# A Fourier-mixing layer with a gated feed-forward: first loads on GpSimd's queue, exponent clamps on GpSimd, 20 products of ones, and a planner with new costs and keys

## The chip, the cores and the metric

One core of one Trainium2 chip runs the kernel. The metric is the device time in microseconds. Three runs of the kernel before took 1538.30, 1540.07 and 1543.28 us, a median of 1540.07.

## What is computed

x is 8 images of 3136 rows by 256 channels. Each image is transformed along its rows, mixed across channels by a complex matrix, soft-thresholded and transformed back. The 25088 rows then go through a feed-forward of width 1024.

```python
def _attn_ref(x, w_r, w_i, b_r, b_i):
    X = np.fft.rfft(x, axis=1)
    Yr = Xr @ w_r - Xi @ w_i + b_r
    Yi = Xr @ w_i + Xi @ w_r + b_i
    Yr = np.sign(Yr) * np.maximum(np.abs(Yr) - lam, 0.0)      # Yi alike, lam = 0.01
    y = np.fft.irfft(Yr + 1j * Yi, n=x.shape[1], axis=1)

def _moe_ref(x, w_in, w_out, g_ln):
    h = x @ w_in
    solu = h * softmax(h)
    ln = (solu - mu) / np.sqrt(var + 1e-06) * g_ln
    return ln @ w_out
```

## The kernel before, in words

The transform of length 3136 = 98 x 32 is done in two stages with a twiddle between them. For image 0, `fwd1_plain` (L778) takes x in eight chunks of 98 x 1024, multiplies each by the 98 x 98 matrix `fa_s` (fp32, two products of 512 columns a chunk, two instructions a product), copies the results out of PSUM on ScalarE and stores them to DRAM (`s1f`). The four even chunks are loaded on SyncE's queue (tiles `u`), the four odd ones on ScalarE's (tiles `xw`). VectorE takes each chunk's largest magnitude (`peaks`). `x_scale` (L664) turns the eight peaks into one scale: a reduce (`top`), a transpose by TensorE, a reduce (`v`), and in `spread` (L683) a product with a row of ones that puts the value on all partitions, and small VectorE operations that end in the scale `sc[:, 4:]`.

`load_bin` (L818) reads the stored result back in another layout (for image 0 into the `xw` tiles), ScalarE casts it to fp16 and VectorE makes the low half (tile `bin`); `fwd2` (L923) is the second stage with filters `fb`; `mix_first` (L974) multiplies by the mixing matrix (`w_hi`, `w_lo`, 12 products of 512 columns for each of 12 units); `threshold` (L1014) and two GpSimd subtractions (`y<-yt,yc` and `yl<-y,yh`) follow; `inv1` (L1038) is the first inverse stage with filters `gb`, stored to DRAM; `inv2` (L1097) reads it back and makes the rows of the feed-forward (`ring_hi`, `ring_lo`). Of each 128 rows, a head (`ph`, softmax), a turn (cast, transposes by DMA) and a tail (`po`, output) make the result. Image 1's first stage is plain as well; images 2 to 7 use a folded one (`fwd1_fold`).

The feed-forward's weights arrive as 64-bit words, since the host hands them over as doubles. `load_wide` (L619) loads 512 of them per partition and rebuilds fp32: mask the exponent (tile `lh`), two clamps of it (`lh<-lh`, written as `ex`), merge it with the sign (`ll<-u,lh`), build the mantissa (`junk`), and one GpSimd product of the two. There are eight such loads: four for `w_in` (`moe_w_in`, L1315) and four for `w_out` (`moe_w_out`, L1345). `power_of_two` (L1330) makes a scale from their peaks.

The mixing weights w_r and w_i are four loads of 128 x 256 fp32 (tile `zt`), held after an earlier copy in the plan. The constants `gs_s`, `fs_s`, `iaf_s`, `fq_s`, `ia_s` and the filters are loaded by `load_after` (L649) on SyncE's queue. `load` (L594) loads `fa_s`; two more loads on SyncE bring the bias rows. Twelve products of ones run at the start while nothing else is there.

No instruction is issued at once. `Plan` records every operation, weighs it (`weigh`, L408: a length, and for a transfer the bytes on a shared bus), and `order` (L459) simulates the five engines: whenever one is free it takes, among the operations that could start within 50 ns of the earliest, the one with the lowest key. The program is then issued in the order of the simulated starts; on each engine it runs in that order. A key is that of the stage and image (`KEYS`, with a step per unit), plus an offset for stage and image (`SHIFT`) and one for the tile written (`ROLE`). `hold` delays an operation in the plan alone; on the chip only real data and buffers are waited for. `x_scale` of image 1 is the ninth step (n = 8) of stage `a1`: its key before is -75.67 + 8 x 10.825.

Of the kernel before, what the change touches and what calls it, by code (L numbers as in the profile page):

```python
# [18 lines left out]
ALU = mybir.AluOpType  # L19
# [225 lines left out]
class Banks:  # L245
# [49 lines left out]
    "b4": -0.33, "b6": 1.62, "a5": 2.05, "b5": -2.17, "b2": 2.33, "a4": 2.62, "b3": -3.91, "a6": -6.82,  # L295
    "a7": -10.33, "a2": -10.77, "a3": 12.99, "b1": 20.66, "b0": -70.35,
# [3 lines left out]
    "head/ph": -0.29, "w_in1/u": 0.37, "b/bin": 0.51, "a/both": 0.58, "head/u": -0.59, "b/Xl": 0.68,  # L300
    "a/av": 0.68, "a/peaks": 1.29, "b/yl": 1.86, "b/Dgb2": 1.92, "w_in0/u": 2.5, "inv2/last_hi": -3.37,
    "a/hsb": 3.92, "weights/u": 3.99, "a/v": 4.16, "a/un": 4.33, "a/pf": -5.05, "head/m": 5.41,
    "w_out0/lh": 5.94, "b/pf": -6.04, "b/Xh16": -6.25, "w_in0/Du": -6.43, "b/yt": 6.86, "a/xw1": -7.25,
    "turn/junk": 7.47, "b/Xs": -7.58, "inv2/last_lo": -8.25, "b/Dgb3": 8.73, "b/y": -10.12, "b/zs": 10.35,
    "w_in1/ll": 10.7, "w_out/o": 12.33, "b/bin_s16": -13.08, "w_out/wout": 17.67, "turn/ll": 24.16,
    "head/a": 36.36, "a/sc": -39.48, "b/zout": -44.76,
# [19 lines left out]
class Op:  # L326
    def __init__(self, engine, stage, role, seq):
        self.engine, self.stage, self.seq = engine, stage, seq
        self.key = key_of(*stage) + SHIFT.get("".join(map(str, stage[:2])), 0) + ROLE.get(f"{stage[0]}/{role}", 0)
        self.calls, self.length, self.moved, self.tiles = [], 0.0, 0.0, []  # L330
        self.needs, self.next, self.start, self.end, self.half, self.port = set(), [], None, None, False, False
# [7 lines left out]
class Plan:  # L339
# [7 lines left out]
    PACE = 1.006  # L347
# [60 lines left out]
    def weigh(self, op, name, args, kw, ins, outs):  # L408
        if name == "dma_start":
# [3 lines left out]
            op.length += 1600.0 if cross else 430.0  # L413
            op.moved += 1500.0 if cross else size / 270.0
# [8 lines left out]
        else:  # L423
# [11 lines left out]
            if op.engine == "gpsimd" and name == "tensor_scalar":  # L435
                each = 1.15
# [6 lines left out]
            op.length += self.CALL[op.engine] + big * each + max(scalars, 0) * self.SCALAR[op.engine]  # L443
# [15 lines left out]
    def order(self):  # L459
        ready = {e: [] for e in self.ENGINES}  # L460
        free = dict.fromkeys(self.ENGINES, 0.0)
        waits, bus, half, port = {}, 0.0, False, 0.0
# [16 lines left out]
        def may_start(op):  # L479
            at = max(free[op.engine], op.at, port if op.port else 0.0, bus - self.BACKLOG if op.moved else 0.0)  # L480
            taken = {}
            for t in op.tiles:
                if t.owner is None:
                    k = t.kind
                    n = len(k.placed) + taken.get(k, 0)
                    taken[k] = taken.get(k, 0) + 1
                    if turn.get(t, n) != n:
                        return np.inf
                    n -= k.bufs
                    if n >= 0:  # L490
# [76 lines left out]
def fft_mix_solu_kernel(ctx: ExitStack, tc, x, w_r, w_i, b_r, b_i, w_in, w_out, g_ln, fa, fq, none, iaf, fb, fs, gb, gs, ia, out):  # L567
# [35 lines left out]
    for r, v in enumerate((b_r, b_i)):  # L603
        nc.sync.dma_start(bias_row[:, r], v.unsqueeze(0))
# [14 lines left out]
    def load_wide(dst, src, before=None):  # L619
# [17 lines left out]
        nc.vector.tensor_scalar(ex, ex, least, -least, ALU.max, ALU.add)  # L637
        nc.vector.tensor_scalar(ex, ex, float(255 << 20), 8.0, ALU.min, ALU.mult)
# [10 lines left out]
    def load_after(t, src, before):  # L649

        nc.hold(before)
        nc.sync.dma_start(t, src)
# [11 lines left out]
    def x_scale(b):  # L664
# [16 lines left out]
        nc.vector.tensor_scalar(sc[:, 4:], sc[:, :1], S_SCALE, None, ALU.mult)  # L681
# [136 lines left out]
    def load_bin(b, g):  # L818
# [11 lines left out]
        if b == 0 and g == 0:  # L830
            for to, src in ((gs_s, gs), (fs_s, fs), (iaf_s, iaf), (fq_s, fq), (ia_s, ia)):
                load_after(to, src, raw[0, 0])
        if b == 0:
            load_after(fb_s[g], fb[:, g * QG : (g + 1) * QG], raw[0, g - 1] if g else done[0, NCH - 1])
# [642 lines left out]
```

## Time and profile before

| | us |
|---|---|
| median of three runs | 1540.07 |
| the profiled execution's own time | 1535.88 |
| its span, first to last instruction | 1533.9 |
| TensorE busy | 1489.9 |
| VectorE busy | 1226.8 |
| ScalarE busy | 1166.3 |
| GpSimd busy | 1084.9 |

PE is TensorE's products and PEld its weight loads, DVE is VectorE, ACT ScalarE, POOL GpSimd, SPq the queue on SyncE that issues transfers. Nearly every instruction carries the line of one recording helper (L457), so instructions are told apart by their tiles, written out<-in. All PSUM tiles are parts of one tensor, `store`. PEclk is TensorE's granted clock as a share of 2.4 GHz. A product's start is when it began; because products overlap, their steps are better read from the starts than from the durations.

### The profile page before, as it was taken

How to read it: one execution, taken by the hardware profiler on the slowest of the kernel's cores; microseconds unless marked ns; L12 is line 12 of the kernel's file. 1: busy time of each engine (PE TensorE's matmuls, PEld its weight loads, DVE VectorE, ACT ScalarE, POOL GpSimd, SP SyncE). 2: the span in 40 equal slices, each digit the busy share in tenths (PEclk: the TensorE clock that was granted, in tenths of full speed). 3: DMA queues.
4: the chain of work that ended last, by engine and by line, in shares of the span. 5: the costliest groups of instructions: out<-in, count | busy, mean ns of one | idle time of the engine just before them, and what ended most of it. 6: DMA issues, size and time to landing. Idle time of an engine off the chain costs nothing.

```text
span 1533.9 us, 40789 instructions
## 1 busy us (share of the span) xinstructions
PE 1489.9 (97%) x15471; PEld 1036.4 (68%) x15471; DVE 1226.8 (80%) x2571; ACT 1166.3 (76%) x2134; POOL 1084.9 (71%) x1351
## 2 busy tenths in 40 slices
PE   6979999999999999999999999999999999999998
PEld 3436677676666777766677677667777777776666
DVE  4888989888888898888889898777886877776664
ACT  5767877778778877778677787777887877677775
POOL 0555787778767778677876887758887788765665
PEclk8989999999999999999999999999999999999999
DMA  8779868987899889998799998897865955687766
GB/s 242 214 231 227 172 153 178 201 174 176 161 233 197 194 191 207 182 190 183 151 218 200 218 194 194 193 203 153 163 137 125 190 116 132 129 172 147 142 120 120
DMA packets 527312, 273.14 MB, mean 178 GB/s; under 512 B 426752, under 2 KB 505068, under 8 KB 527056
## 3 DMA queue, kind: packets, MB, share of 16 engines
q1 hardware_dynamic: 526668, 268.94, 81.8%
q8 instruction: 121, 1.98, 0.6%
q10 hardware_dynamic: 448, 1.61, 0.4%
q14 instruction: 75, 0.61, 0.1%
HBM read 84.71 MB, written 82.97 MB: 109 GB/s over the span
## 4 chain that ended last, share of the span: by engine, by line
PE 51%; DVE 3%; ACT 1%; issue 1%; POOL 1%; DMA 1%; SPq 0%; DVEq 0%; ACTq 0%; POOLq 0%
PE store L457 51%; DMA xw<-in_x_dram 1%; POOL ll L457 1%; DVE m L457 1%; DVE u L457 0%; ACT u L457 0%; ACT lh L457 0%; DVE bin L457 0%; DVE peaks L457 0%; DMA th<-lh 0%; SPq L457 0%; DVE yt L457 0%; DVE xw L457 0%; POOL r L457 0%; ACT junk L457 0%
## 5 line engine op out<-in xcount | busy, mean ns | idle before, releaser
L457 POOL TENSOR_TENSOR ll<-u,lh 128x1024 f16<-128x1024 f32 x196 | 422.6, 2157 | 162.8 <-ACT lh L457 147.6
L457 PE MATMUL store<-wout,th 128*128 128x256 f16 x3136 | 374.8, 273 | 5.0 <-DVE Xl L457 1.5
L457 PEld LDWEIGHTS <-th 128*128 128x128 f16 x3136 | 303.0, 98 | 65.1 <-issue 10.6
L457 DVE TENSOR_REDUCE m<-store 128x1 f32<-128x1024 f32 x196 | 239.1, 1220 | 94.1 <-PE store L457 93.2
L457 DVE SCALAR_TENSOR_TENSOR u<-store,ch,u 128x1024 f32<-128x1024 f32 x196 | 250.9, 1280 | 74.0 <-ACT u L457 71.8
L457 ACT CAST lh<-u 128x1024 f16<-128x1024 f32 x196 | 205.8, 1051 | 121.3 <-DVE u L457 66.4
L457 PE MATMUL store<-win_hi,ring_hi 128*128 128x512 f16 x768 | 291.3, 379 | 3.5 <-DVE u L457 2.9
L457 PE MATMUL store<-win_low,ring_lo 128*128 128x512 f16 x768 | 291.0, 379 | 0.0
L457 PE MATMUL store<-win_lo,ring_hi 128*128 128x512 f16 x768 | 291.0, 379 | 0.0
L457 ACT ACTIVATE u<-store,m,hsb 128x1024 f32<-128x1024 f32 x192 | 231.6, 1206 | 76.8 <-DVE m L457 73.5
L457 PEld LDWEIGHTS <-ring_hi 128*128 128x128 f16 x1536 | 148.2, 98 | 148.3 <-issue 11.5
L457 ACT ACTIVATE junk<-u,su 128x1024 bf16<-128x1024 f32 x196 | 226.6, 1156 | 3.4 <-DVE u L457 3.3
L457 PE MATMUL store<-wout,tl 128*128 128x256 f16 x1568 | 203.4, 273 | 1.7 <-DMA tl<-ll 1.7
L457 PEld LDWEIGHTS <-tl 128*128 128x128 f16 x1568 | 151.6, 98 | 27.7 <-issue 3.4
L457 PE MATMUL store<-w_hi,Xh 128*128 128x256 f16 (+1 forms) x584 | 165.4, 283 | 3.5 <-ACT Xh L457 1.3
L457 PE MATMUL store<-w_hi,Xl 128*128 128x256 f16 (+1 forms) x584 | 165.3, 283 | 0.6 <-DVE Xl L457 0.3
L457 PE MATMUL store<-w_lo,Xh 128*128 128x256 f16 (+1 forms) x584 | 165.2, 283 | 0.0
L457 POOL TENSOR_TENSOR y<-yt,yc 128x512 f32<-128x512 f32 (+1 forms) x104 | 128.9, 1241 | 29.3 <-ACT yt L457 26.3
L457 PEld LDWEIGHTS <-Xh 128*128 128x128 f16 x1168 | 112.7, 98 | 37.1 <-issue 11.0
L457 PEld LDWEIGHTS <-ring_lo 128*128 128x128 f16 x768 | 75.1, 98 | 90.7
L457 POOL TENSOR_TENSOR yl<-y,yh 128x512 f16<-128x512 f32 x96 | 112.8, 1179 | 18.5 <-ACT yh L457 18.1
L457 ACT ACTIVATE o<-store,r 128x256 f32<-128x256 f32 x196 | 93.3, 477 | 40.3 <-PE store L457 36.9
(178 smaller groups left out, 2468.8 us busy)
## 6 DMA issues: line engine op xcount, KB each, us to landing
s<-av SPq DMA_DIRECT2D x48, 512.0 KB
zt<-s SPq DMA_DIRECT2D x56, 392.0 KB
s<-zout SPq DMA_DIRECT2D x42, 512.0 KB
xw<-in_x_dram SPq DMA_DIRECT2D x48, 384.0 KB
bin<-s SPq DMA_DIRECT2D x72, 256.0 KB
out_dram<-o SPq DMA_DIRECT2D x128, 96.0 KB
out_dram<-o SPq DMA_DIRECT2D x136, 64.0 KB
out_dram<-o SPq DMA_DIRECT2D x128, 32.0 KB
```

The costliest lines, as they stand in the source:

```text
L457: getattr(engine, name)(*args, **kw)
```

## The change

The matrix `fa_s`, the two bias rows, the mixing weights, the five constants and the first filter block are issued on GpSimd's queue. Two of the four exponent operations of each wide load run on GpSimd. Twenty more products of ones are put on TensorE once image 0's scale is there. The planner counts at most eight transfers in flight on the hardware queues, has other lengths for transfers and for GpSimd's operations, and all keys differ.

```diff
-    "fa": -300, "bias": -243.29, "start": 0, "warm": -200, "plain": -200, "weights": -203.16, "consts": -100,
-    "groups": 0, "x0": -175.82, "y0": -51.96, "b0": -115.32, "b0s": 4.277, "w_in0": -161.15, "w_in1": -112.71,
-    "w_in": -109.53, "w_out0": -71.07, "w_out": -17.01, "mix": 116.28, "pads": -69.29, "a1": -75.67,
-    "a1s": 10.825, "a2": 18.06, "a2s": 1.034, "a": 0.49, "b1": -21.98, "b1s": 1.959, "b": 2.06, "bs": 1.538,
-    "inv2": -85.41, "turn": 153.65, "tail": 3.96, "as": 1.842,
+    "fa": -300, "bias": -279.1, "start": 0, "warm": -200, "plain": -200, "weights": -170.64, "consts": -100,
+    "groups": 0, "x0": -159.35, "y0": -57.88, "b0": -127.06, "b0s": 2.121, "w_in0": -171.39, "w_in1": -140.45,
+    "w_in": -126.15, "w_out0": -114.06, "w_out": -71.7, "mix": 30.93, "pads": -77.8, "a1": -130.39,
+    "a1s": 16.887, "a2": -19.92, "a2s": 1.248, "a": -1.85, "b1": -27.4, "b1s": 1.388, "b": -1.43, "bs": 1.393,
+    "inv2": -132.6, "turn": 153.08, "tail": 3.75, "as": 1.384, "again": -154.07,
 SHIFT
-    ... "a3": 12.99, "b1": 20.66, "b0": -70.35,
+    ... "a3": 11.28, "b1": 30.66, "a1": -37.21, "b0": -65.91,
 ROLE (37 offsets in place of 37 others)
 Plan
+    LANES = 8
+    LAND = 2300.0
-    PACE = 1.006
+    PACE = 1.003
 weigh, a transfer
-            op.length += 1600.0 if cross else 430.0
-            op.moved += 1500.0 if cross else size / 270.0
+            soft = op.engine == "gpsimd"
+            op.length += 1400.0 if cross else 1000.0 if soft else 530.0
+            op.moved += 700.0 if cross else size / 270.0
+            op.lane = not soft
 weigh, a GpSimd operation
+            if op.engine == "gpsimd" and name == "tensor_scalar":
+                each = 345.0 if big == 1 else 140.0 + big * 1.15
 may_start
+            if op.lane and len(lands) >= self.LANES:
+                at = max(at, lands[-self.LANES])
 order
-                op.end = bus + 2000.0
+                op.end = bus + self.LAND
+                if op.lane:
+                    lands.append(op.end)
 load; the bias rows
-        nc.sync.dma_start(t, src)
+        nc.gpsimd.dma_start(t, src)
-        nc.sync.dma_start(bias_row[:, r], v.unsqueeze(0))
+        nc.gpsimd.dma_start(bias_row[:, r], v.unsqueeze(0))
 load_wide
-        nc.vector.tensor_scalar(ex, ex, least, -least, ALU.max, ALU.add)
-        nc.vector.tensor_scalar(ex, ex, float(255 << 20), 8.0, ALU.min, ALU.mult)
+        nc.gpsimd.tensor_scalar(ex, ex, least, -least, ALU.max, ALU.add)
+        nc.gpsimd.tensor_scalar(ex, ex, float(255 << 20), 8.0, ALU.min, ALU.mult)
 load_after
-        nc.sync.dma_start(t, src)
+        (queue or nc.sync).dma_start(t, src)
 x_scale, image 0
-        nc.vector.tensor_scalar(sc[:, 4:], sc[:, :1], S_SCALE, None, ALU.mult)
+        nc.hold(nc.vector.tensor_scalar(sc[:, 4:], sc[:, :1], S_SCALE, None, ALU.mult))
+        nc.at("again")
+        pw = banks.tile("po")
+        with nc.together():
+            for k in range(20):
+                nc.tensor.matmul(pw[:, :P], ones, ones, start=k == 0, stop=k == 19)
 load_bin: gs, fs, iaf, fq, ia, and fb of block 0
-                load_after(to, src, raw[0, 0])
+                load_after(to, src, raw[0, 0], nc.gpsimd)
 the mixing weights
-            load_after(w3[h][:, j], w[h * P : (h + 1) * P], done[0, 3])
+            load_after(w3[h][:, j], w[h * P : (h + 1) * P], done[0, 3], nc.gpsimd)
```

## Rows read from the trace of the kernel before

**Rows 1.** The page: TensorE's busy time, share of the span, instructions.

```profile
PE 1489.9 (97%) x15471; PEld 1036.4 (68%) x15471; DVE 1226.8 (80%) x2571; ACT 1166.3 (76%) x2134; POOL 1084.9 (71%) x1351
```

**Rows 2.** Stretches of the run: busy time by engine, granted clock, DMA.

```profile
core 0: us, PE busy (x) PEld busy (x) DVE busy (x) ACT busy (x) POOL busy (x), PEclk, DMA share, GB/s
6.47:26.87 20.40, 19.42 (x45) 7.92 (x46) 10.11 (x10) 11.33 (x22) 2.79 (x4) 0.92 0.87 264
26.87:45.00 18.13, 8.25 (x79) 3.70 (x79) 12.89 (x37) 11.33 (x21) 0.00 (x0) 0.63 0.77 228
45.00:96.00 51.00, 48.10 (x689) 24.00 (x686) 43.81 (x72) 40.20 (x79) 35.67 (x29) 1.00 0.77 231
96.00:108.00 12.00, 3.02 (x26) 0.73 (x9) 11.58 (x26) 8.19 (x15) 3.92 (x4) 0.66 0.77 251
130.00:900.00 770.00, 755.53 (x8200) 532.06 (x8206) 664.23 (x1374) 602.11 (x1108) 577.96 (x712) 1.00 0.90 189
900.00:1520.00 620.00, 620.00 (x6278) 443.31 (x6261) 465.29 (x999) 476.09 (x858) 456.10 (x590) 1.00 0.76 156
```

**Rows 3.** TensorE's timeline, first 41 us: start, duration, instruction, [idle before <-releaser].

```profile
1.34 4.36 PE L457 MATMUL store<-ones 128*128 128x128 f32 x24 [1.34 <-DVE mhalf L457]
6.47 1.96 PE L457 MATMUL store<-xw,fa_s 98*98 98x512 f32 x4 [0.77 <-DMA xw<-in_x_dram]
...
11.06 3.65 PE L457 MATMUL store<-u,fa_s 98*98 98x512 f32 x4 [0.72 <-DMA u<-in_x_dram]
14.98 1.96 PE L457 MATMUL store<-u,fa_s 98*98 98x512 f32 x4 [0.26 <-DMA u<-in_x_dram]
...
28.46 0.62 PE L457 MATMUL store<-v,ones 1*128 1x1 f32 x4 [1.12 <-DVE v L457]
35.62 0.29 PE L457 MATMUL store<-fb,bin 64*128 64x64 f16 x4 [6.54 <-ACT bin L457]
36.94 1.35 PE L457 MATMUL store<-fb,bin 64*128 64x64 f16 x44 [1.03 <-DVE bin L457]
...
39.87 0.63 PE L457 MATMUL store<-w_lo,Xh 128*128 128x512 f16 x1
40.30 0.62 PE L457 MATMUL store<-w_hi,Xl 128*128 128x512 f16 x1
```

**Rows 4.** SyncE's queue, timeline of issues: start, time to issue, transfer.

```profile
0.72 0.44 SPq L457 DMA_DIRECT2D fa_s<-in_fa_dram  x1
...
1.80 6.76 SPq L457 DMA_DIRECT2D u<-in_x_dram  x4
...
26.91 0.34 SPq L457 DMA_DIRECT2D s1f<-tl  x1
...
30.46 2.04 SPq L457 DMA_DIRECT2D xw<-s1f  x4
```

**Rows 5.** Stretches of 2 us around the first hole, columns as in rows 2.

```profile
30.00:32.00 2.00, 0.00 (x0) 0.00 (x0) 2.00 (x7) 2.00 (x7) 0.00 (x0) 0.91 0.16 48
32.00:34.00 2.00, 0.00 (x0) 0.00 (x0) 1.43 (x4) 1.85 (x7) 0.00 (x0) 0.50 0.91 314
...
44.00:46.00 2.00, 2.00 (x52) 1.13 (x51) 0.75 (x1) 0.14 (x1) 0.00 (x0) 0.68 0.86 233
```

**Rows 6.** TensorE's timeline from 94 to 118 us.

```profile
108.01 0.32 PE L457 MATMUL store<-ident,top 98*1 98x98 f32 x1 [6.58 <-DVE top L457]
108.12 6.30 PE L457 MATMUL store<-xw,fa_s 98*98 98x512 f32 x8
```

**Rows 7.** VectorE's timeline: image 0's last scale; the clamp nearest to `top`.

```profile
29.32 0.15 DVE L457 TENSOR_SCALAR sc<-sc 128x1 f32<-128x1 f32 x1
...
105.34 0.41 DVE L457 TENSOR_SCALAR lh<-lh 128x512 uint32<-128x512 uint32 x1
```

**Rows 8.** Tile `lh` from 40 to 131 us: ns min/median/max, first and last start.

```profile
L457 DVE TENSOR_SCALAR lh<-lh x16: 410/414/834, 49.2 to 110.6; 128x512 uint32<-128x512 uint32 x16
```

**Rows 9.** GpSimd's groups over the run: busy us, mean ns, idle before.

```profile
L457 POOL TENSOR_TENSOR y<-yt,yc 128x512 f32<-128x512 f32 x96 | 122.5, 1277 | 29.2 <-ACT yt L457 26.3
...
L457 POOL TENSOR_SCALAR yc<-yt,sc 128x512 f32<-128x512 f32 x84 | 68.1, 812 | 24.2 <-DVE yt L457 19.3 <-DVE ch L457 3.5 <-DVE un L457 0.8
```

More of the change, by code (lines that the diff above doesn't have):

```diff
@@ L292 @@
+    "groups": 0, "x0": -159.35, "y0": -57.88, "b0": -127.06, "b0s": 2.121, "w_in0": -171.39, "w_in1": -140.45,
+    "w_in": -126.15, "w_out0": -114.06, "w_out": -71.7, "mix": 30.93, "pads": -77.8, "a1": -130.39,
+    "a1s": 16.887, "a2": -19.92, "a2s": 1.248, "a": -1.85, "b1": -27.4, "b1s": 1.388, "b": -1.43, "bs": 1.393,
+    "inv2": -132.6, "turn": 153.08, "tail": 3.75, "as": 1.384, "again": -154.07,
 }
 SHIFT = {
-    "b4": -0.33, "b6": 1.62, "a5": 2.05, "b5": -2.17, "b2": 2.33, "a4": 2.62, "b3": -3.91, "a6": -6.82,
@@ L296 @@
-    "a7": -10.33, "a2": -10.77, "a3": 12.99, "b1": 20.66, "b0": -70.35,
+    "b5": -0.34, "a6": 2.88, "a7": 6.98, "b2": 7.05, "b4": 7.45, "a5": 7.96, "a4": 9.2, "a3": 11.28, "b1": 30.66,
+    "a1": -37.21, "b0": -65.91,
 }
 ROLE = {
-    "head/ph": -0.29, "w_in1/u": 0.37, "b/bin": 0.51, "a/both": 0.58, "head/u": -0.59, "b/Xl": 0.68,
-    "a/av": 0.68, "a/peaks": 1.29, "b/yl": 1.86, "b/Dgb2": 1.92, "w_in0/u": 2.5, "inv2/last_hi": -3.37,
-    "a/hsb": 3.92, "weights/u": 3.99, "a/v": 4.16, "a/un": 4.33, "a/pf": -5.05, "head/m": 5.41,
@@ L303 @@
[L303 to L306, printed above, removed]
+    "tail/po": 0.15, "head/ph": -0.17, "w_in0/u": 0.4, "b/Dxw0": 0.46, "b/bin": 0.6, "a/sc": 0.72,
+    "turn/r": -0.79, "head/u": -1.18, "a/v": -1.49, "head/m": 1.55, "w_in1/lh": 1.69, "head/ch": -1.89,
@@ L307 @@
+    "a/bias_y": 1.98, "a/both": 2.12, "b/Xl": -2.31, "a/top": 3.09, "a/xw0": 3.16, "weights/u": -4.1,
[3 rows of a table added]
+    "w_in1/ll": 20.29, "a/peaks": 25.23, "head/a": 36.79, "b/zout": -55.1,
 }
@@ L330, in __init__ @@
         self.calls, self.length, self.moved, self.tiles = [], 0.0, 0.0, []
-        self.needs, self.next, self.start, self.end, self.half, self.port = set(), [], None, None, False, False
+        self.needs, self.next, self.start, self.end, self.half, self.port, self.lane = set(), [], None, None, False, False, False
     def touch(self, tile):
@@ L434, in weigh @@
                 each = 2.12
-            if op.engine == "gpsimd" and name == "tensor_scalar":
-                each = 1.15
             if op.engine == "vector" and sbuf and name in ("tensor_scalar", "tensor_copy") and big > 1:
@@ L442, in weigh @@
                 op.port = True
-            op.length += self.CALL[op.engine] + big * each + max(scalars, 0) * self.SCALAR[op.engine]
+            each = self.CALL[op.engine] + big * each + max(scalars, 0) * self.SCALAR[op.engine]
+            if op.engine == "gpsimd" and name == "tensor_scalar":
+                each = 345.0 if big == 1 else 140.0 + big * 1.15
+            op.length += each
             if "accum_out" in kw and op.engine == "scalar":
@@ L461, in order @@
         free = dict.fromkeys(self.ENGINES, 0.0)
-        waits, bus, half, port = {}, 0.0, False, 0.0
+        waits, bus, half, port, lands = {}, 0.0, False, 0.0, []
         for op in self.ops:
@@ L647, in fft_mix_solu_kernel, with load_after @@
     s1 = {}
-    def load_after(t, src, before):
+    def load_after(t, src, before, queue=None):
         nc.hold(before)
-        nc.sync.dma_start(t, src)
+        (queue or nc.sync).dma_start(t, src)
     xw = [const.tile([P, 2 * C1], F32, name=f"xw{i}") for i in range(2)]
@@ L831, in load_bin @@
             for to, src in ((gs_s, gs), (fs_s, fs), (iaf_s, iaf), (fq_s, fq), (ia_s, ia)):
-                load_after(to, src, raw[0, 0])
+                load_after(to, src, raw[0, 0], nc.gpsimd)
         if b == 0:
-            load_after(fb_s[g], fb[:, g * QG : (g + 1) * QG], raw[0, g - 1] if g else done[0, NCH - 1])
+            load_after(fb_s[g], fb[:, g * QG : (g + 1) * QG], raw[0, g - 1] if g else done[0, NCH - 1], None if g else nc.gpsimd)
             load_after(gb_s[g].rearrange("p u r t m -> p u (r t) m"), gb[:, g * QG // 2 : (g + 1) * QG // 2].rearrange("p u r t m -> p u (r t) m"), raw[b, g])
```

3 rows, old and new, of the table ROLE are left out of this document.

## The prediction

> **What bounds the kernel now.** I read the page first, then stretches of the run, then TensorE's own rows where it stands still, then the queue or engine that it waits for. On the page TensorE is busy for 1489.9 of 1533.9 us [rows 1]. So about 44 us are all that any reordering can win from waiting, plus what TensorE loses while its granted clock is at half. The stretches show where those are [rows 2]. From 900 to 1520 us TensorE never waits. From 130 to 900 it waits 14.5 us. The rest lies in the first 108 us, in two holes. In the first (26.87 to 45.00) it is busy 8.25 of 18.13 us at a mean clock of 0.63; in the second (96 to 108) 3.02 of 12 us at 0.66. After each hole the time lost is not made up, because TensorE has work queued behind it without a break; what is saved there comes off the end nearly one for one.
>
> The first hole is a round trip. TensorE's last product before it is the spread of image 0's scale at 28.46; the next starts at 35.62, when ScalarE has cast the first block read back from DRAM [rows 3]. That block's load is issued at 30.46, after the last store at 26.91 has landed [rows 4]. The granted clock falls in the middle of the hole: 0.91 from 30 to 32 us, 0.50 from 32 to 34, and 0.68 only from 44 to 46 [rows 5], that is from 2.4 to 1.2 GHz until some 9 us after work resumed.
>
> The second hole is TensorE's queue held up by one instruction. The transpose of image 1's peak (`top`) waits 6.58 us for VectorE and starts at 108.01; eight first-stage products stand behind it and run at half clock [rows 6].
>
> **The change, part by part.** The sum is made against the profiled execution, 1535.88 us (span 1533.9 and 2.0 outside it); the median of the three runs shown, 1540.07, lies 4.2 above it. I put the differences on the median.
>
> *Loads on GpSimd's queue.* The DFT matrix and two bias rows leave SyncE's queue, so its first load of x is issued at 0.72 in place of 1.80 [rows 4]: 1.08 us sooner. TensorE waits for that load at 11.06 and for the next at 14.98, and runs without a break from there to the end of the stage [rows 3]. At 11.06 the four products also take 3.65 us, against 1.96 for the same four at 14.98. At best the stage gains 1.08 + 1.69 = 2.8 us. Against it: the mixing weights (4 loads of 128 KB) move to GpSimd's queue too. Their hold on an earlier copy orders the plan only and is no wait on the chip; nothing stands before them in GpSimd's queue but the matrix and the biases, so they go out while x is still coming. 524 KB at the stage's 264 GB/s [rows 2] are 2.0 us. I take the middle of -2.8 and +2.0: **-0.4**. The matrix itself: GpSimd's queue shows no load in this trace. On SyncE it is issued at 0.72 and first needed at 6.47 [rows 4, 3]. The move costs between 0 (it still lands in time) and 5.7 us (it takes that long once more); as the product of 6.47 waits for x, I take 0. The five later constants, the first filter block and the weights are 10 issues fewer on SyncE; I take 0, since SyncE waits from the issue at 26.91 to 30.46 for the store to land, whatever stood before. Were that cover gone, they would be worth an issue of some 0.4 us each.
>
> *Ones products.* 20 fp32 products of 128x128 are 40 instructions; 24 such take 4.36 us at the start [rows 3], so these take 7.27. They are held by the last scale of image 0, which the trace shows at 29.32 to 29.47 [rows 7]. They end near 36.74. TensorE's queue is in order, so the four products of 35.62 wait behind them, and all of image 0's chain behind those; but the next 44 wait for VectorE until 36.94 anyway [rows 3]. I price the delay at +0.1 (bounds 0 and +1.1, the whole 36.74 - 35.62). In return the clock should still be full when the mix starts: its products follow each other at 0.43 us now (39.87, 40.30 [rows 3]), at half clock; twelve of them at full clock save 12 x 0.215 = 2.6. Bounds: 0 if the chain behind is bound elsewhere, 4.1 if all of the 8.25 us that TensorE is busy in that hole [rows 2] were halved. Sum of this part **-2.5**.
>
> *Clamps on GpSimd.* Eight wide loads each give up two VectorE clamps; the sixteen have a median of 0.414 us [rows 8]: 6.6 us off VectorE. The last of four such clamps ahead of `top` starts at 105.34 [rows 7], and VectorE is busy 11.58 of the 12 us of that hole [rows 2], so `top` comes 4 x 0.41 = 1.6 us sooner. On GpSimd I take 0.81 us each, from its threshold operation of the same shape; its two-input subtract of 1.28 is the upper bound [rows 9]. That is 13 us (at most 20) in stretches where GpSimd is idle 15.3 us before 96 us and 8.1 us in the hole [rows 2]. The price is a new wait: VectorE's sign merge now waits for two GpSimd operations, and behind it stand the low halves and peaks for which TensorE waits; on GpSimd, the subtractions of image 0's mix stand behind the clamps, and the inverse stage waits for these. I cost those at 0, since GpSimd's idle time covers them.
>
> *Plan and keys.* The new costs and keys reorder all five queues. What that gives cannot be read from rows; only its bounds can. In the second hole the whole loss is 9.0 us of idle and 2.9 us of half clock (the eight products of 108.12 take 6.30, at full clock about 8 x 0.43 [rows 6, 3]), 11.9 together. The last step of image 1's front, which makes `top`, moves from key +10.9 (-75.67 + 8 x 10.825) to -32.5, ahead of the first heads, which suggests a smaller hole. The weights of the output layer move ahead as well (-71 to -114), which keeps VectorE full. Bounds for this hole: -11.9 and +1.6 (below, the port). I take the clamps' 1.6 and half of the 4.94 us that remain of the wait: **-4.1**. In the long stretch after 130 us I take 0, with bounds of -14.5 (all waiting there gone) and +13.2 (two waits like the 6.58).
>
> Sum: -0.4 - 2.5 - 4.1 + 0 = **-7.0**, so 1533.1 us for the median (1528.9 against the profiled execution). A difference of 0.3%, 4.6 us, is about what a measurement of this kernel tells from no change.
>
> **The rivals.** (1) *The second hole closes.* The keys put enough work before `top`, and its wait and half clock go altogether: -6.6 - 2.9 in place of -4.1; with the full lead of the first load this is -2.8 - 2.5 - 9.5 = -14.8, **1525.3**. For it: VectorE alone holds that wait. Against: work that could fill it also waits for VectorE or for image 0's own round trip.
>
> (2) *GpSimd's clamps block VectorE.* The clamp on VectorE varies from 0.410 to 0.834 us [rows 8]: something doubles it at times. If each of the four clamps before `top` holds VectorE for its 0.81 us, VectorE loses 3.2 us and gains 1.6: +1.6 in place of -4.1, sum -1.3, **1538.8**. The Trainium skill states such a rule (SBUF — State Buffer, section Who interferes with whom): VectorE's two-port and two-input SBUF instructions and GpSimd share a port pair as an exclusive lock, and the second to issue blocks. The spread of 0.410 to 0.834 agrees with it, but the median of 0.414 says that it is rare so far.
>
> (3) *Slower: the new order opens holes in the long stretch.* The mechanism is that of the second hole: an image's peak transpose, put into TensorE's queue before VectorE has got to it, stops everything behind it. Each image from 2 to 7 has one. Two waits of 6.58 us would be +13.2: -7.0 + 13.2 = +6.2, **1546.3**. It decides once TensorE's waits between 130 and 900 us exceed today's 14.5 by 11.6. For it: VectorE is busy 86% there [rows 2] and every key of those steps is changed. Against: today's order shows the wait only once.
>
> (4) *The ones do not hold the clock.* If it is at half before they start, 40 of them take 14.5 us, to 44.0, and the 44 products of 36.94 come 7.1 us late: -0.4 + 7.1 - 4.1 = +2.6, **1542.7**. Against: they start 0.4 us after the products of 28.46 end, and the clock is still at 0.91 from 30 to 32.
>
> **How the numbers follow.** Forecast 0.42, rivals (1) 0.22, (2) 0.18, (3) 0.14, (4) 0.04. The forecast and (1) lie over 4.6 us below: faster 0.64. (2) and (4) lie within it: same 0.22. (3): slower 0.14. The range is 1521 to 1545: below, it takes in (1) with some of the long stretch's waits gone too; above, (2), (4) and the near side of (3). The likeliest case's own range is 1529 to 1535.4.
>
> **What would show it.** In the changed profile: an x load on SyncE at about 0.7 us; 40 ones products starting near 29 us with the clock at 1.00 through 45 us, and the mix's products 0.215 us apart; lh clamps in GpSimd's rows at about 0.8 us and none in VectorE's; TensorE's longest wait on `top` under 5 us and its clock less than 15 us at half near 100 us; TensorE's waits from 130 to 900 us near 14.5. I am wrong if the weights' loads push the first stage's end past 27 us, if the mix is no faster although the clock holds, if VectorE's two-input operations lengthen between 45 and 115 us, or if a new wait of several us appears after 130 us.

## The result and the profile after

The kernel after takes **1561.87 us** (median of four runs, 1560.28 to 1562.17). The kernel before took 1539.18 us beside it (four runs). The ratio is 1.014 with a 95% interval of 1.012 to 1.016: 22.7 us slower, where 7.0 us faster was forecast, and above the range. The profiled execution has a span of 1560.2 us. Its page, answering [rows 1]: 40 more TensorE instructions, 14.6 us more busy time, and 11.7 us more idle time.

```profile
PE 1504.5 (96%) x15511; PEld 1048.4 (67%) x15511; DVE 1222.2 (78%) x2555; ACT 1167.4 (75%) x2134; POOL 1129.1 (72%) x1380
```

Stretches of the kernel after, columns as in [rows 2]:

```profile
core 0: us, PE busy (x) PEld busy (x) DVE busy (x) ACT busy (x) POOL busy (x), PEclk, DMA share, GB/s
...
29.57:45.00 15.43, 7.67 (x89) 6.16 (x88) 9.01 (x26) 8.68 (x17) 0.00 (x0) 0.77 0.84 258
45.00:96.00 51.00, 43.48 (x568) 20.70 (x568) 38.53 (x50) 32.88 (x64) 41.92 (x27) 0.94 0.56 169
96.00:108.00 12.00, 11.80 (x98) 5.66 (x96) 8.56 (x17) 9.84 (x20) 10.55 (x10) 1.00 0.80 264
108.00:130.00 22.00, 10.45 (x64) 3.98 (x65) 14.98 (x27) 11.35 (x22) 20.09 (x13) 0.69 0.77 215
130.00:200.00 70.00, 63.29 (x388) 41.81 (x390) 59.17 (x152) 51.03 (x96) 46.05 (x58) 0.90 0.85 189
200.00:900.00 700.00, 689.95 (x7690) 491.02 (x7683) 591.53 (x1206) 542.87 (x998) 531.25 (x640) 1.00 0.88 184
```

TensorE is busy 43.48 us from 45 to 96 us where it was 48.10; GpSimd (POOL) is busy 41.92 us there where it was 35.67. The hole of 96 to 108 us is gone, and there is another from 108 to 130. From 200 to 900 us TensorE waits 10.1 us; in the kernel before TensorE is busy 689.29 us of the same stretch, so it waits 10.7. The first product of the first head is the mark that I use below: it starts at 139.81 us, before at 117.81, so 22.0 of the span's 26.3 us are lost ahead of it (the profiled execution of before lies 4.2 under its median, this one at its own).

TensorE's timeline of the first 131 us, answering [rows 3] and [rows 6]:

```profile
9.17 2.44 PE L462 MATMUL store<-xw,fa_s 98*98 98x512 f32 x4 [2.33 <-DMA fa_s<-in_fa_dram]
...
26.77 0.25 PE L462 MATMUL store<-ident,top 98*1 98x98 f32 x1
...
28.07 4.73 PE L462 MATMUL store<-ones 128*128 128x128 f32 x40
32.64 1.89 PE L462 MATMUL store<-u,ones 128*128 128x256 f32 x8
...
40.46 0.29 PE L462 MATMUL store<-fb,bin 64*128 64x64 f16 x4 [4.14 <-ACT bin L462]
...
44.31 0.61 PE L462 MATMUL store<-w_hi,Xh 128*128 128x512 f16 x1 [1.18 <-ACT Xh L462]
...
129.53 3.71 PE L462 MATMUL store<-iaf_s,zt 98*128 98x98 f32 x16 [8.40 <-DMA zt<-s2f]
```

Three things are to be seen. The first product comes late (9.17 for 6.47), and it is the matrix that is waited for. The 40 ones instructions take 4.73 us and stand *ahead* of the column sums of the mixing weights (`u,ones`), which start at 32.64; so the first product of the next stage comes at 40.46 for 35.62 and the first of the mix at 44.31. And the longest wait is now 8.40 us, at 129.53, for a load of `zt` from `s2f`: image 0's first inverse stage, stored and read back. That load is issued on SyncE's queue at 125.07, in the kernel before at 106.05.

The tile `lh` of the kernel after (answering [rows 8]: engine, count, ns min/median/max), and then GpSimd's timeline:

```profile
L462 POOL TENSOR_SCALAR lh<-lh x16: 1929/1938/2923, 50.5 to 130.7; 128x512 uint32<-128x512 uint32 x16
```

```profile
50.47 3.98 POOL L462 TENSOR_SCALAR lh<-lh 128x512 uint32<-128x512 uint32 x2 [28.51 <-DVE lh L462]
54.53 1.77 POOL L462 TENSOR_TENSOR y<-yt,yc 128x512 f32<-128x512 f32 x1
...
83.97 3.94 POOL L462 TENSOR_SCALAR lh<-lh 128x512 uint32<-128x512 uint32 x2
87.88 1.16 POOL L462 TENSOR_TENSOR yl<-y,yh 128x512 f16<-128x512 f32 x1
89.12 1.98 POOL L462 TENSOR_SCALAR lh<-lh 128x512 uint32<-128x512 uint32 x1
91.18 1.26 POOL L462 TENSOR_TENSOR y<-yt,yc 128x512 f32<-128x512 f32 x1
...
117.12 0.72 POOL L462 TENSOR_TENSOR yh<-y,yh 64x256 f16<-64x256 f32 x1
```

A moved operation takes 1.94 us, not 0.81, and 33.0 us for all 16. They stand between the subtractions (`y`, `yl`, `yh`) of image 0's mix. The last of these ends the chain that the inverse stage waits for: it starts at 117.12. In the kernel before it started at 99.65 and the first inverse product at 114.26, with no wait, as the timelines of GpSimd and of TensorE have it:

```profile
99.65 1.14 POOL L457 TENSOR_TENSOR yh<-y,yh 64x256 f16<-64x256 f32 x1 [3.16 <-ACT yh L457]
```

```profile
114.26 3.71 PE L457 MATMUL store<-iaf_s,zt 98*128 98x98 f32 x32
```

### The profile page after: what moved, and what is told of

Its sections match the earlier page's. It is cut to its first block, busy times and chain, and to the rows that moved or that the text cites. A ratio compares the mean times of both kernels' runs of the same rounds, so it can differ in the third digit from the quotient of the medians.

```text
span 1560.2 us, 40898 instructions
## 1 busy us (share of the span) xinstructions
PE 1504.5 (96%) x15511; PEld 1048.4 (67%) x15511; DVE 1222.2 (78%) x2555; ACT 1167.4 (75%) x2134; POOL 1129.1 (72%) x1380
## 4 chain that ended last, share of the span: by engine, by line
PE 77%; POOL 6%; DMA 5%; ACT 4%; DVE 4%; issue 2%; SPq 1%; POOLq 0%; ACTq 0%; DVEq 0%
PE store L462 77%; POOL lh L462 2%; POOL y L462 1%; DMA tl<-ll 1%; POOL yl L462 1%; ACT u L462 1%; SPq L462 1%; DVE u L462 1%; DMA th<-lh 1%; DMA zt<-s 1%; POOL ll L462 1%; DMA bin<-s 1%; DVE m L462 1%; DMA out_dram<-o 1%; DMA xw<-s1f 1%
```

## The experiments

Differences are against the median of the kernel before, run beside each group (1535.98 for the runs e, 1538.68 for f1 and f3 to f5, 1539.45 for f2, f6, f8 and f9, 1538.45 for g1 to g3, 1537.99 for g4 and g5).

### First round: one part undone, and planned anew

e1 is the kernel after with the two operations back on VectorE; e4 the kernel before with them on GpSimd; e5 the kernel after with a planner that knows their length. In each the planner orders everything again.

```diff
e1  -        nc.gpsimd.tensor_scalar(ex, ex, least, -least, ALU.max, ALU.add)
e1  +        nc.vector.tensor_scalar(ex, ex, least, -least, ALU.max, ALU.add)
e4  the reverse, in the kernel before; both: the second operation alike
e5  -                each = 345.0 if big == 1 else 140.0 + big * 1.15
e5  +                each = 345.0 if big == 1 else 140.0 + big * (3.5 if ins[0].dtype == U32 else 1.3)
e6  -        nc.gpsimd.tensor_scalar(ex, ex, least, -least, ALU.max, ALU.add)
e6  +        nc.gpsimd.tensor_scalar(exf, exf, 0.5, 0.0, ALU.max, ALU.add)
```

Expected of e1:

> The changed kernel with the two clamps of each wide load back on VectorE; all else as changed, the plan made anew. Theory C (clamps): sixteen clamps take 1.94 us each on GpSimd, 31 us, and stand in its queue ahead of image 0's subtractions; without them the first product of a feed-forward head comes at 120 to 126 us in place of 139.8, and the time falls from 1561.9 to about 1545 (1540 to 1550). Rival K (keys, loads and ones make the delay, the clamps only lie beside it): the first head stays past 134 us and the time within 5 us of 1562.

Measured: 1576.32 us, +40.3 (ratio 1.0257, 1.0236 to 1.0277).

Expected of e4:

> The kernel before with only the two clamps moved to GpSimd, keys and loads as before. Theory C: the clamps alone cost most of the change, 10 to 20 us, so 1549 to 1560, with the first head past 127 us. Rival K: the old keys leave room for them beside other work, within 5 us of the kernel before. If the port alone were the matter, VectorE's operations between 45 and 115 us would lengthen and nothing wait for GpSimd.

Measured: 1577.78 us, +41.8 (1.0264, 1.0247 to 1.0282).

Expected of e5:

> The changed kernel, with the plan told that an integer clamp of 512 columns takes 1.93 us on GpSimd (it reckons 0.73). Rival O (the order is at fault: the plan puts the clamps ahead of subtractions because it takes them for short): the plan moves them behind, and at least half of the 17 us come back, 1545 to 1553. Theory C in its plain form (31 us of work are too much for GpSimd in that stretch, in any order): at most a third comes back, 1556 to 1564.

Measured: 1583.93 us, +48.0 (1.0309, 1.0294 to 1.0324).

None of these says what it was made for. In e1 the first head came 10.9 us sooner than in the kernel after (128.9 us), and the rest took 25.7 us longer. The planner, given one other engine or length, puts TensorE's instructions in another order far beyond the part under test. From the first head to the end e4 takes 1444.9 us and e5 1451.6, where the two kernels take 1416.1 and 1420.4. What these three show is that: with the keys as they are, each new plan cost 25.7 to 31.2 us from the first head to the end. For the price of a part the order has to stay.

e6 changes no length in the plan. It runs the two operations on fp32 views of the same tile, with other constants, so that the weights of the feed-forward take other values.

Expected of e6:

> The changed kernel with the clamps on GpSimd working on float views of the same words, with other constants, so the feed-forward's weights get other values of a sane size. Queue, places and waits are the same; only the length should differ. If the integer type makes the length, a clamp takes about 0.8 us in place of 1.94, as the float threshold does (0.83); then theory C puts the first head near 125 us and the time near 1547. Rival (the two immediate operands or the place make the length): 1.9 us and 1562 again. Rival P (what hurts is the wait between VectorE and GpSimd, not the length): 0.8 us, but within 5 us of 1562.

Measured: 1563.76 us, +27.8 (1.0174, 1.015 to 1.0199), and the row of tile `lh` in e6:

```profile
L462 POOL TENSOR_SCALAR lh<-lh x16: 1922/1932/2927, 52.5 to 134.3; 128x512 f32<-128x512 f32 x16
```

The type is not what makes them long.

### Second round: the planned order kept, one part changed where instructions are issued

The plan is made as it was; after it, a marked operation goes to another engine's queue at its place, or is left out. The other instructions of every engine keep their order.

```diff
f, g         -                engine = getattr(self.nc, op.engine)
f, g         +                engine = getattr(self.nc, getattr(op, "on", op.engine))
f1 (after)   +        (nc.gpsimd.tensor_scalar(ex, ex, least, -least, ALU.max, ALU.add)).on = "vector"
f4 (before)  +        (nc.vector.tensor_scalar(ex, ex, least, -least, ALU.max, ALU.add)).on = "gpsimd"
f3 (after)   the 20 ones products are left out of the issued order
f2 (after)   +        nc.gpsimd.dma_start(t, src).on = "sync"       # the matrix; the bias rows alike
f5 (after)   f1, f2 and f3 together
g1 (after)   f5, and load_after's transfers .on = "sync" too
```

Expected of f1:

> The changed kernel in its own planned order, every engine's sequence kept, with only the sixteen clamps issued on VectorE at the places where the plan had them on GpSimd. The replanned version of this lost 26 us behind the first head, which the plan and not the clamps may have done. Theory C (clamps): the first head comes 10 to 16 us earlier than 139.8 and what follows it keeps its 1420 us, so 1546 to 1552. Rival K (keys and their order): the same order gives the same holes, the time stays within 4 us of 1562. Rival R (any departure from the tuned order costs over 10 us behind the first head): slower than 1562.

Measured: 1549.37 us, +10.7 (1.0071, 1.0043 to 1.01). The kernel after stands at +22.7, so the move is worth 12.0 of it. The stretch of 45 to 96 us of f1, columns as in [rows 2]:

```profile
45.00:96.00 51.00, 49.64 (x649) 23.48 (x648) 45.63 (x68) 40.01 (x76) 33.21 (x25) 0.97 0.68 207
```

Expected of f4:

> The kernel before in its own planned order, with only the sixteen clamps issued on GpSimd. The replanned version was 42 us slower. Theory C: the clamps themselves cost 10 to 18 us, so 1546 to 1556, all of it before the first head (117.8 before). Rival K: under 5 us. If it is 42 us again, the clamps cost that much in any order and the replanning nothing.

Measured: 1564.08 us, +25.4 (1.0166, 1.0139 to 1.0193). The same stretch of f4, and then TensorE's waits from 28 to 142 us (us in total, times, longest):

```profile
45.00:96.00 51.00, 38.76 (x532) 18.86 (x537) 33.37 (x46) 28.65 (x53) 40.48 (x27) 0.87 0.56 166
```

```profile
PE store L460 <- DVE top L460: 11.8, 1, 11.8
PE store L460 <- POOL yl L460: 7.7, 3, 4.4
```

The move done alone slows the kernel before by more than the whole change does, TensorE waits for GpSimd's `yl`, and the wait for `top`, which the move was to shorten, grows from 6.6 to 11.8 us.

Expected of f3:

> The changed kernel in its own order without the twenty products of ones. Theory S (the ones stand in TensorE's queue ahead of the column sums of the mixing weights, which start at 32.64 in place of about 28.1, and so hold up the weights' scale, the casts on ScalarE behind it and the first mix): without them the first mix product comes 3 to 4.5 us earlier than 44.31 and the time falls by 3 to 4.5. Rival H (they hold the clock): the mix runs at half clock for longer and the gain is under 1 us, or a loss.

Measured: 1556.88 us, +18.2 (1.0116, 1.009 to 1.0143): the ones cost 4.5 us. TensorE's timeline of f3: the weights' sums start at 28.46 and the mix 4.07 us sooner than in the kernel after, its products still 0.43 us apart.

```profile
28.46 1.99 PE L465 MATMUL store<-u,ones 128*128 128x256 f32 x8
...
40.24 0.61 PE L465 MATMUL store<-w_hi,Xh 128*128 128x512 f16 x1 [1.18 <-ACT Xh L465]
```

Expected of f2:

> The changed kernel in its own order with only the matrix and the two bias rows issued on SyncE again. TensorE waits 2.3 us for the matrix in the changed kernel and starts its first real product at 9.17. Theory M (that wait is on the path): the first product comes at 6.3 to 7, and 1 to 2.5 us come off 1561.9. Rival N (x arrives no sooner, so TensorE waits for x in its place): under 1 us. The runs without the ones (-5.0) and with all three parts undone leave about 1 us for it.

Measured: 1560.97 us, +21.5 (1.014, 1.0111 to 1.0168). TensorE's timeline of f2 moves by more than the time does:

```profile
5.49 1.88 PE L465 MATMUL store<-xw,fa_s 98*98 98x512 f32 x4
...
24.16 0.25 PE L465 MATMUL store<-ident,top 98*1 98x98 f32 x1
...
41.71 0.61 PE L465 MATMUL store<-w_hi,Xh 128*128 128x512 f16 x1 [1.18 <-ACT Xh L465]
```

The stage ends 2.6 us sooner (24.16 for 26.77), the mix starts 2.6 us sooner, and the first head only 1.5 (138.34), as GpSimd's last subtraction does (115.66 for 117.12), which suggests that GpSimd's queue, more than the start, sets the pace between. Single profiles differ by as much here: the transpose of image 0's `top` starts at 27.09 in the kernel before, at 25.39 in f8 and at 28.74 in f4, with the same instructions ahead of it. The 1.2 us between the two kernels lie within both intervals.

Expected of f5:

> The changed kernel in its own order, with the clamps on VectorE, without the ones, and with the matrix and the biases on SyncE. What is left of the change are the keys, the plan's costs and the later loads on GpSimd. If the three parts make the whole loss, the time is 1535 to 1542, that of the kernel before. If the keys lose by themselves, it stays over 1545; if they win what they were planned to, it is under 1535.

Measured: 1543.39 us, +4.7 (1.0035, 1.0018 to 1.0052). The three parts taken singly sum to 12.0 + 4.5 + 1.2 = 17.7 us, together 18.0: they add. The time lies between the expectations: the three parts are most of the loss and not all of it.

Expected of g1:

> The kernel after with its order as planned, but with the clamps on VectorE, no second set of ones products, and every load that the change moved back on SyncE's queue: what is left of the change is the order itself (keys and planner). The theory that the order alone costs the residue of +4 to +5 us: 1543 to 1545 beside a kernel before of 1539 (ratio 1.003 to 1.004), with TensorE waiting 8 to 10 us for zt from s2f. The rival, that the residue is the ten later loads on GpSimd's queue: 1539 to 1541, within 0.15% of the kernel before.

Measured: 1541.33 us, +2.9 (1.0029, 1.0009 to 1.0049). So the new order by itself costs about 3 us, and the later loads on GpSimd's queue are the difference of f5 and g1, 1.8 us, which the intervals don't separate from 0. The time lies between the two expectations. TensorE's timeline of g1, and the issue of the load that is waited for, on SyncE's queue:

```profile
97.32 0.24 PE L465 MATMUL store<-ident,top 98*1 98x98 f32 x1 [0.75 <-DVE top L465]
...
118.79 3.74 PE L465 MATMUL store<-iaf_s,zt 98*128 98x98 f32 x16 [10.89 <-DMA zt<-s2f]
```

```profile
114.22 0.74 SPq L465 DMA_DIRECT2D zt<-s2f  x2
```

The same load in the kernel before:

```profile
106.05 0.74 SPq L457 DMA_DIRECT2D zt<-s2f  x2
```

The wait for `top` is 0.75 us where it was 6.58, as the keys' order suggested. But now the round trip of image 0's first inverse stage is waited for, 10.89 us. Before, the products held up by `top` ran until 114.26, and by then `zt` had landed. The round trip itself also comes later: in g1 the mix starts 3.8 us sooner than before (35.67 for 39.47), but the last subtraction 5.0 us later (104.65 for 99.65) and the load 8.2 us later. So the order loses its time between the mix and this load, in the stretch in which it puts image 1's peak 10.7 us forward (97.32 for 108.01). No run tells apart which of the keys does it.

### Third round: parts alone in the order of before

f8 is the kernel before with the 20 ones, told to the planner as of no length; f9 the kernel before with the weights', the five constants' and the first filter's loads on GpSimd's queue.

```diff
f8  +        nc.at("again")
f8  +                nc.tensor.matmul(pw[:, :P], ones, ones, start=k == 0, stop=k == 19)
f9  +        nc.sync.dma_start(t, src).on = queue
```

Expected of f8:

> The kernel before, in its own order, with only the twenty products of ones, held by image 0's scale; the sums of the mixing weights stand ahead of them here. This is what the prediction priced at -2.5: they fill the hole from 29 to 35.6 us, the clock stays at full through the first mix, whose products then follow each other at 0.215 us. Expected 1535 to 1538, with the clock at 1.00 from 30 to 46 us. Since forty of them took 4.73 us and not 7.27, they end near 34 us and the clock may still fall before the mix; then no change within 2 us (rival).

Measured: 1542.75 us, +3.3 (1.0021, 1.0005 to 1.0038). TensorE's timeline of f8:

```profile
26.77 0.61 PE L461 MATMUL store<-v,ones 1*128 1x1 f32 x4 [1.12 <-DVE v L461]
27.31 4.73 PE L461 MATMUL store<-ones 128*128 128x128 f32 x40
34.04 0.23 PE L461 MATMUL store<-fb,bin 64*128 64x64 f16 x4 [2.00 <-ACT bin L461]
...
39.89 0.47 PE L461 MATMUL store<-w_hi,Xh 128*128 128x512 f16 x1
40.20 0.38 PE L461 MATMUL store<-w_lo,Xh 128*128 128x512 f16 x1
40.41 0.38 PE L461 MATMUL store<-w_hi,Xl 128*128 128x512 f16 x1
```

Here the ones stand where the prediction had them, behind the weights' sums. Half clock still comes, later and for less time: the mix's products step by 0.43 us up to 39.89 and by 0.215 from 40.20 on. The first head starts at 116.25, 1.6 us sooner than before, and the time is not shorter. That lead is not the ones' doing: the products ahead of them (`v,ones`) already start 1.7 us sooner than in the kernel before (26.77, [rows 3]: 28.46), whose profiled execution ran at half clock from 11 to 15 us (0.54 and 0.61) where this one ran at full. From `v,ones` to the end of the first twelve mix products f8 takes 14.6 us and the kernel before 16.2, a gain of 1.6 us. From `v,ones` to the first head both take the same (89.5 and 89.4 us), so that gain is lost again in between.

Expected of f9:

> The kernel before, in its own order, with only the mixing weights, the five constants and the first filter block issued on GpSimd's queue; matrix and biases stay on SyncE. If these loads go out at once and take bandwidth from x, the last first-stage product ends later than 25.4 us and the time rises by 1 to 2 us. If they only relieve SyncE, the hole from 29 to 35.6 us shrinks a little: -1 to 0 us. Either way within 3 us of the kernel before.

Measured: 1541.89 us, +2.4 (1.0014, 1.0 to 1.0027): no gain. The second chunk on SyncE's queue is waited for a little longer (1.60 us, [rows 3]: 0.26), but f8, which moves no load, waits 1.30 us for it, so this says nothing of the loads.

### Fourth round: what the moved operations cost by their form

All four keep the order of the kernel that they are made from. f6 computes the same values as the kernel after, with max and min in the first operation and add and multiply in the second. g2 and g3 leave out the max and the min, and add or multiply alone. g4 and g5 leave them out too, in the form add, then multiply.

```diff
f6  +        nc.gpsimd.tensor_scalar(ex, ex, least, least + float(255 << 20), ALU.max, ALU.min)
f6  +        nc.gpsimd.tensor_scalar(ex, ex, -least, 8.0, ALU.add, ALU.mult)
g2  +        nc.gpsimd.tensor_scalar(ex, ex, -least, None, ALU.add)
g2  +        nc.gpsimd.tensor_scalar(ex, ex, 8.0, None, ALU.mult)
g4  +        nc.gpsimd.tensor_scalar(ex, ex, -least, 8.0, ALU.add, ALU.mult)
g4  +        nc.gpsimd.tensor_scalar(ex, ex, 0.0, 1.0, ALU.add, ALU.mult)
g3, g5  as g2 and g4, in the kernel before
```

Expected of f6:

> The changed kernel in its own order; the same clamp values come out, but the first of the two GpSimd operations now does maximum and minimum and the second addition and multiplication. Float words took 1.93 us as well, so the type is not it. If the pair of operations makes the length, the first takes about 0.8 us as the threshold's minimum and maximum do, the second 1.9 or more, and the time falls by 4 to 7 us. If immediate operands make it (the threshold's bounds come from tiles), both take 1.9 us and the time stays within 3 us of 1562.

Measured: 1553.80 us, +14.4 (1.0097, 1.0072 to 1.0122). GpSimd's timeline of f6:

```profile
67.32 1.91 POOL L465 TENSOR_SCALAR lh<-lh 128x512 uint32<-128x512 uint32 x1
69.31 1.16 POOL L465 TENSOR_TENSOR yl<-y,yh 128x512 f16<-128x512 f32 x1
70.56 0.62 POOL L465 TENSOR_SCALAR lh<-lh 128x512 uint32<-128x512 uint32 x1
```

The first operation (max and min) takes 1.91 us, the second (add and multiply) 0.62. The expectation had it the other way round.

Expected of g2:

> The kernel after with its order as planned; the two GpSimd operations of each wide load do the add and the multiplication alone and leave out the max and the min. The theory that the price of the max and min forms is what the clamps' move cost: each operation takes 0.62 us (1.94 in the kernel after), the 16 take 10 us in place of 33, and the time falls to 1548 to 1552, where the clamps on VectorE brought it (1549.4 beside 1538.7). The rival, that any two GpSimd operations between VectorE's mask and its merge cost the same by the two hand-overs: 1558 to 1562.

Measured: 1558.31 us, +19.9 (1.0138, 1.0112 to 1.0164). One operation alone is not the short form: its median is 1.50 us. So the time is the rival's, but the run does not test the rival: the operations were not short.

Expected of g3:

> The kernel before with its order as planned; the two operations of each wide load run on GpSimd as in g2 (the add and the multiplication alone, without max and min). If cheap GpSimd operations relieve VectorE as the prediction had it: the wait for top falls from 6.6 to about 5 us and the time is 1536 to 1539, up to 3 us under the kernel before. The rival, that the kernel before has no room on GpSimd in its first 130 us even at 0.62 us: 1541 to 1546, with waits for yl or yh of 2 us or more.

Measured: 1558.35 us, +19.9 (1.0133, 1.0109 to 1.0157). Both expectations rest on 0.62 us; here the operations take 1.68 in the mean, and TensorE waits 10.3 us for `top`.

Expected of g4:

> The kernel after with its order as planned; both moved operations of each wide load are of the form add, then multiply, with the max and the min left out. Each should take 0.62 us, as the add and multiply form did in f6, so the 16 take 10 us. The theory that the price of the GpSimd forms sets the loss (mean of 2.06 us: 1561.9; 1.63: 1558.3; 1.33: 1553.8; on VectorE: 1549.4): 1547 to 1550, as with the operations on VectorE. The rival, that the hand-over to GpSimd costs by itself: 1552 to 1555.

Measured: 1549.78 us, +11.8 (1.0072, 1.0056 to 1.0088). The row of tile `lh` in g4, and the last subtraction of image 0 in GpSimd's timeline:

```profile
L465 POOL TENSOR_SCALAR lh<-lh x16: 617/617/988, 50.2 to 115.2; 128x512 uint32<-128x512 uint32 x16
```

```profile
105.77 1.17 POOL L465 TENSOR_TENSOR yh<-y,yh 64x256 f16<-64x256 f32 x1 [1.04 <-issue]
```

Expected of g5:

> The kernel before with its order as planned; the same two add and multiply operations, without max and min, run on GpSimd. By price alone, 0.62 us each: 1538 to 1543 beside a kernel before of 1539, with waits for yl under 2 us. The rival, that the order of before has no room on GpSimd between 45 and 110 us: 1545 to 1552. A relief of VectorE that pays would show as under 1537.

Measured: 1542.07 us, +4.1 (1.0025, 1.0009 to 1.0041), as by price alone. TensorE's longest wait for `yl` is 1.4 us, and its wait for `top` is 7.7 us.

Set side by side, in the two orders:

| where and how the 16 operations run | mean, us | last subtraction of image 0 starts | first head starts | difference |
|---|---|---|---|---|
| order of after: as changed | 2.06 | 117.12 | 139.81 | +22.7 |
| g2, one operation each | 1.63 | 116.38 | 137.12 | +19.9 |
| f6, max and min, then add and multiply | 1.33 | 112.39 | 133.10 | +14.4 |
| g4, add and multiply | 0.65 | 105.77 | 127.48 | +11.8 |
| f1, on VectorE | 0.52 | 107.10 | 129.23 | +10.7 |
| order of before: f4, as changed | 2.11 | 115.67 | 141.47 | +25.4 |
| g3, one operation each | 1.68 | 111.47 | 134.03 | +19.9 |
| g5, add and multiply | 0.75 | 101.39 | 120.98 | +4.1 |
| the kernel before, on VectorE | 0.46 | 99.65 | 117.81 | 0 |

In both orders the time follows the duration of the operations. In the order of after, at 0.65 us, the move costs what it costs on VectorE, within the intervals, so there the hand-over to GpSimd is not what it pays for. In the order of before a small price is left at 0.75 us (+4.1, interval 1.4 to 6.3), and whether it is the duration or the hand-over isn't shown. The move gains nothing either: g4 is no faster than f1, and g5 is slower than the kernel before.

## Why the prediction was wrong

**Clamps on GpSimd** is the step that failed, twice. "I take 0.81 us each, from its threshold operation of the same shape" with 1.28 as the upper bound: measured 1.94 us, 2.06 in the mean, beyond both ends. The row had the shape and not the form: the threshold takes its bounds from a tile, in the order min, max, and writes another tile, while these take constants and write in place. The pair of operations matters (f6: 1.91 against 0.62 us) and the type does not (e6); which of the other differences parts the threshold from max and min with constants, no run tells. And "I cost those at 0, since GpSimd's idle time covers them": 15.3 us of idle time before 96 us were an average over a queue that works in order, and the operations stood in it between image 0's subtractions, which the prediction had named as the work behind them. At their true length they do not fit by amount either: 33.0 us, against 23.4 us of idle time that the prediction counted. The chain runs from the clamps to the last subtraction (17.5 us later than before, 10.0 of them by the move, since f1 has it at 107.10), the inverse stage, its store and load, and TensorE's wait at 129.53. The two faults are one price: by the runs it is 12.0 us in the order of after and 25.4 in that of before; with 0.65 us each it is about 1 (g4 against f1), with 0.75 in the order of before 4.1. The expected 1.6 us of relief for VectorE never showed: the wait for `top` grew from 6.6 to 11.8 us in f4, and even in g5 to 7.7.

**Second hole, -4.1.** The mechanism named was right: the keys put work before `top`, and its wait fell to 0.75 us in g1 and to 0.2 in the kernel after, where TensorE's timeline has it:

```profile
107.34 0.24 PE L462 MATMUL store<-ident,top 98*1 98x98 f32 x1 [0.16 <-DVE top L462]
```

What failed is that the 6.58 us would come off the end. The wait for `top` lay over the round trip of image 0's inverse stage (99.65 to 114.26, 14.6 us), and when it went, that was waited for instead, 10.9 us in g1. An estimate of what could have come off: in g1 and in the kernel after the product starts 4.5 us after the load's issue, so before, with the load issued at 106.05, it could have started near 110.6 in place of 114.26, 3.7 us sooner at best. The step asked what holds the queue and not what is late next. The order by itself came to +2.9 us, where its share of the -4.1 was -2.5 and the clamps' the other 1.6.

**Ones, -2.5.** The length was mis-sized the cheap way (4.73 us, not 7.27: the 24 of [rows 3] ran at half clock for most of their time, 0.213 us apart up to 4.3 us and 0.112 from 4.4 on, while the 40 ran at full), and the place was wrong. The prediction kept the weights' sums ahead of them. The plan had put the sums behind them, so that VectorE's weight scale, ScalarE's casts and the bins came late: the mix started at 44.31 for 39.47, and f3 takes 4.07 us of these 4.84 off. Nor did the clock hold: TensorE then waits, 4.14 us of it for `bin`, and the granted clock falls to half. Stretches of 2 us of the kernel after, columns as in [rows 2]:

```profile
36.00:38.00 2.00, 0.32 (x2) 0.24 (x2) 1.65 (x6) 1.99 (x5) 0.00 (x0) 0.96 1.07 344
38.00:40.00 2.00, 0.00 (x0) 0.00 (x0) 1.87 (x7) 2.00 (x5) 0.00 (x0) 0.50 1.13 280
```

So +4.5 us. Even in the right place (f8) 1.6 us were gained by the end of the first mix products and gone by the first head: this is the prediction's own bound of 0, "if the chain behind is bound elsewhere". By what, these runs don't settle.

**Loads, -0.4.** SyncE's first load went out at 0.72 as forecast. The 1.69 us that the stage was to gain at 11.06 were half clock (0.54 and 0.61 from 11 to 15 us), and the kernel after has it again (0.50 from 11 to 13). The matrix, "as the product of 6.47 waits for x, I take 0", was the value at the wrong end of 0 to 5.7: TensorE waited 2.33 us for it. The page of the kernel after gives its way from issue to landing (the last number, us):

```profile
fa_s<-in_fa_dram POOLq DMA_DIRECT2D x1, 37.5 KB, 7.8
```

The matrix cost 1.2 us by f2, the loads after it 1.8 by f5 and g1, both smaller than their intervals.

**Long stretch, 0.** Right as far as single profiles tell: from the first head to the end 1420.4 us, before 1416.1, and four runs of the kernel before spread over 5.1 us. The third rival, which was the one on the slower side, named this stretch, and so it had the right sign by luck, for the wrong place. Its fear came true in e1, e4 and e5, where the plan was new and the keys were not.

**Rival (2)**, the port: VectorE's eight masks (`lh<-u`) between 45 and 130 us went from 476 to 706 ns in the mean, by three of the eight. The Trainium skill's rule (SBUF — State Buffer, section Who interferes with whom) would give that, an exclusive lock, and these rows agree: the three ran beside a GpSimd instruction. But the two longest (1.37 and 1.38 us) ran beside subtractions and only one (0.82) beside a moved operation, and f1, with the operations on VectorE, has one of 1.38 too. The price of the port for the end isn't told apart here; VectorE had idle time there, and in g4 the masks took 599 ns with no more time than f1's within the intervals. **Rival (4)**, that the clock is not held, came out in part, by the wait behind the ones and not by half clock ahead of them.

Sum: 12.0 (clamps) + 4.5 (ones) + 1.2 (matrix) + 1.8 (later loads) + 2.9 (order) = 22.4 of 22.7 us. The terms of 1 to 3 us carry intervals as wide as themselves. Open: which keys make the order alone slower by 2.9, and what takes back the 1.6 us gained at the mix in f8. No version that was run beats the kernel before.

## What to carry to other kernels

Price a moved instruction by a row of the same engine with the same pair of operations and the same kind of operands, and where none exists let the upper bound reach to a few times the nearest. Idle time in a queue that works in order covers a new instruction only if nothing behind it is on the path: list what stands there. Before a wait is booked as a gain, find the wait that it hides, and to test one part of a planned kernel, keep the planned order and change only where the instruction is issued.

## What the runs showed of the hardware

GpSimd's two-operation form with constants on 128x512 took 0.62 us for add then multiply, 1.91 for max then min, 1.94 for max with add or min with multiply, and 1.50 for add or multiply alone; with bounds from a tile, min and max took 0.81 in fp32 [rows 9]. The element type made no difference (1.93 us in fp32). The Trainium skill (GPSIMD Engine Reference, section 3.1) has VectorE about twice as fast in an elementwise add; here VectorE's 0.42 us for the kernel's one-input form stands against 0.62 for the best of these forms (1.5 times) and 1.94 for the kernel's own (4.6 times). A 37.5 KB load on GpSimd's queue took 7.8 us from issue to landing beside x's loads and another of that size (`iaf_s`) 2.2 us later on, and each such issue held GpSimd for 0.5 to 0.8 us. Forty ones instructions at full clock took 4.73 us, 0.118 each. The 24 at the start took 4.36 us in the kernel before and 5.49 in the kernel after, where they were 0.213 us apart to the end.
